# A weight gradient of a strided convolution: fifteen direct tap sums replaced by pairs of taps that share a product

## The chip, the cores and the metric

The program runs on one core of one Trainium2 chip. The metric is the device time of one execution in microseconds (us). Before the change it is 2222.19 us, the median of 4 runs (2219.1 to 2223.2). Lower is better.

The engines have short names here. PE is the matrix engine and PEld its weight loads, DVE the vector engine, ACT the scalar engine, POOL the engine GpSimd, and SP the engine whose queue issues most of the transfers (DMAs).

## The reference, cut to what matters

Two convolutions over time, each with 15 taps, a GELU and a stride of 2, are followed by a small joint network. The kernel computes the output and the gradients of all seven inputs.

```python
def _fwd_reference(x, w1, w2, g, w_f, w_g, w_o):
    B, T, D = x.shape            # 2, 4000, 512
    K = w1.shape[0]              # 15 taps
    pad = K // 2
    ...
    h = _gelu(h)[:, ::2, :]      # first convolution with w1, then every 2nd step
    T1 = h.shape[1]              # 2000
    hp = jnp.pad(h, ((0,0),(pad,pad),(0,0)))
    f = jnp.zeros_like(h)
    for i in range(K):
        f = f + jnp.einsum("btc,cd->btd", hp[:, i:i+T1, :], w2[i])
    f = _gelu(f)[:, ::2, :]      # 1000 steps are kept
    ...
def reference(x, w1, w2, g, w_f, w_g, w_o, grad_out):
    _out, _vjp = jax.vjp(_f, x, w1, w2, g, w_f, w_g, w_o)
    return (_out, *_vjp(grad_out))
```

The change concerns one of these gradients, that of `w2` (output `out_3`, 15 x 512 x 512). With `dy` the gradient before the second GELU (1000 kept steps, 512 channels, 2 batches) it is, for each tap `i`, `gw2[i][c, d] = sum over b, t of hp[b, 2t + i, c] * dy[b, t, d]`: fifteen matrix products that contract over 2 x 1000 time steps.

## The kernel before, in words

The kernel is one long program of five stages: (1) first convolution, (2) second convolution, (3) joint network and its gradients, (4) backward through the second convolution, (5) backward through the first. Stage 4 ends with the gradient of `w2`, and this is the part that changes; it is called the w2 stage here. Stage 5 begins with the gradient of `x` and ends with the gradient of `w1`.

**Order.** The program is written in the order of the stages, but a list scheduler orders the instructions of each engine: it goes through the program with a model of durations, and where the next instruction of an engine isn't ready it puts a later one that is ready before it. On the chip each engine then works its own list in order. Most buffers are blocks of one big SBUF tile (`arena`), given out by a first-fit allocator (`_Arena`, L28); an instruction waits for another where their bytes overlap, so an instruction of a new block waits for the last reader of what lay there before. PSUM has two pools in stage 4, 6 banks for sums (`ps_acc`) and 2 for transposes (`ps_tp`).

**The w2 stage.** The hidden activations `h` lie in DRAM (`HD`), channels on partitions, split by the parity of the time step. `dy` is transposed first: `DFP` (L916 to L928) has 125 groups of 8 consecutive steps, the group on the partition, the step `l` in 0..7 and the 512 channels in the free dimension. Then the stage goes through 8 pieces (L951), 2 parities `par` times 4 blocks of 128 channels `cc`. For each piece:

- `load_htr` (L942) brings 504 KB of `h` into `HTr`, two pieces ahead. The buffers alternate, and the SP queue issues the load.
- `deint` (L167, run by `evac` at L163) rearranges it on ACT to `HTd`, two copies of 128 x 1008.
- 32 transposes on PE (L966) turn it to `HN`, time groups on partitions, 16 positions for each batch; 4 PSUM tiles of 8 transposes are emptied by ACT and DVE in turn (L968).
- For each tap of this parity (8 or 7), 16 matmuls (2 batches x 8 steps, L977) of 125 x 128 by 125 x 512 are summed in one bank. The bank is copied to `st` by ACT or DVE (L981), and `st` is stored to `out_3` by the SP queue (L982).

That is 15 taps x 4 blocks x 16 = 960 matmuls and 8 x 32 = 256 transposes.

**Work of stage 5 that is put in between.** `p5w_setup` (L540) allocates the weight buffers of stage 5 and loads the first quarter of `w1` (1920 KB, L447). POOL then forms 7 sums of taps (L448, L449). `p5w_emit` (L548) transposes a loaded quarter (88 transposes, L460) and loads the next; it is called after pieces 2 and 5. `p5x_load` (L509) loads parts of `x` on POOL's queue for the end of stage 5, as soon as the bytes of its blocks are free.

**The function that the change calls.** Stage 5 computes the gradient of `w1` with `kara_wgrad` (L804). It handles the taps in pairs. For taps `t0` and `t0+2` and for even and odd steps of `dy` it makes three sums instead of four: Q from the unchanged data with `dy` even + odd, P and R from differences of neighbouring data with `dy` even and `dy` odd. Then tap `t0` is P + Q and tap `t0+2` is Q - R. Each sum takes half as many matmuls as a direct tap, since it goes over step pairs. ACT copies Q (L825), DVE adds (L827) and subtracts (L831). Tap 13 is left over and is summed directly from two sums in one bank (L843).

Blocks of the arena at the w2 stage, worked out from the allocator's calls (bytes of a partition): DFP 40192 to 56576, HN 56576 to 72960, HTr 72960 to 81024, st 81024 to 84096, the weights for stage 5 143360 to 210944. The stage before had the G1 tile of batch 1 at 101248 to 117248, read last by L894, and weights at 62720 to 85248, read last by L482. Stage 5 puts the two halves of its `x` data at 68416 to 91968 and 91968 to 115520, and SQ where DFP was.

## Time and profile before

| | us |
|---|---|
| time, median of 4 runs | 2222.19 (2219.1 to 2223.2) |
| the profiled execution, its time | 2217.83 |
| the profiled execution, its span | 2216.1 |
| first and last start of the w2 stage's matmuls (L977) | 1275.2 and 1522.1 |
| first and last start of the matmuls of `kara_wgrad` in stage 5 (L820) | 1891.3 and 2184.7 |
| mean granted PE clock over the span | 0.988 |

The span runs from the first to the last instruction; the time has some 1.7 us more. A group's row names the line, engine and operation, output and input, sizes and count, then busy time, the mean of one in ns and the idle time of the engine before it, with what ended that idle time. A row of the timeline has start, duration, engine, line and tiles, and in brackets the idle time before it. A row of the chain has start, duration and what ran. A row of windows gives, for a stretch, each engine's busy time and count, then the granted clock, the DMA share and GB/s. The line named for a copy or a PSUM emptying is that of the helper (L163 for ACT, L165 for DVE).

### The profile page before, as it was taken

What the parts mean: (1) busy time and instruction counts of PE and PEld (TensorE: products, weight loads), DVE (VectorE), ACT (ScalarE), POOL (GpSimd) and SP (SyncE); (2) the same over time, 40 slices, a digit from 0 to 9 for tenths busy, and PEclk for the clock granted to TensorE, in tenths of its full rate; (3) what the DMA queues carried; (4) which work ended last, traced back from release to release, by engine and by line L of the source; (5) the groups of instructions that cost most, each with busy time, mean ns of one, the idle gap of its engine ahead of it and who ended that gap; (6) DMA issues with size and microseconds to landing.
All of it is one profiled execution on the core that took longest, in us unless ns stands there. A gap on an engine that the chain in (4) does not pass through costs nothing.

```text
span 2216.1 us, 29813 instructions
## 1 busy us (share of the span) xinstructions
PE 2116.0 (95%) x12176; PEld 1077.5 (49%) x12176; DVE 796.1 (36%) x1918; ACT 577.7 (26%) x1141; POOL 478.6 (22%) x416
## 2 busy tenths in 40 slices
PE   5999999999899999999799899999999989999999
PEld 4444444444566656666444444444454444444444
DVE  4333433543455555556354511112222242311310
ACT  2112121121555545552221333221122141000000
POOL 0332232353544444443110011011010000100000
PEclk9999999999999999999899899999999999999999
DMA  7422523743222222224210242113121001600000
GB/s 167 100 62 64 137 55 82 179 97 82 89 75 75 76 77 75 77 72 141 89 36 1 59 120 81 36 65 75 26 56 28 19 19 28 135 24 27 27 24 24
DMA packets 227985, 154.16 MB, mean 70 GB/s; under 512 B 167792, under 2 KB 219412, under 8 KB 223592
## 3 DMA queue, kind: packets, MB, share of 16 engines
q1 hardware_dynamic: 221096, 124.09, 21.6%
q0 software_dynamic: 4288, 11.78, 2.4%
q10 hardware_dynamic: 2464, 16.39, 2.3%
q8 instruction: 95, 1.56, 0.3%
q14 instruction: 42, 0.34, 0.1%
HBM read 100.02 MB, written 52.17 MB: 69 GB/s over the span
## 4 chain that ended last, share of the span: by engine, by line
PE 84%; ACT 7%; DVE 4%; DMA 2%; issue 1%; SPq 1%; POOL 0%; ACTq 0%; DVEq 0%; POOLq 0%
PE acc_l L221 22%; PE acc_gw L977 9%; PE acc_bP L482 7%; PE acc_bQ L482 7%; PE acc_bR L482 6%; PE gwo L695 5%; PE pj L677 5%; PE acc_kP L820 4%; PE acc_kR L820 4%; PE acc_kQ L820 4%; ACT arena L163 4%; ACT arena L628 3%; DVE arena L165 2%; PE tp_wk L460 2%; PE pdfe L688 1%; PE acc_k L843 1%
## 5 line engine op out<-in xcount | busy, mean ns | idle before, releaser
L221 PE MATMUL acc_l<-arena 128*128 128x500 bf16 x2208 | 495.2, 385 | 3.1 <-POOL arena L209 1.6
L221 PEld LDWEIGHTS <-arena 128*128 128x128 bf16 x2208 | 213.2, 97 | 283.8 <-issue 5.2
L482 PEld LDWEIGHTS <-arena 128*128 128x128 bf16 x2208 | 211.7, 97 | 256.1 <-DVE arena L165 1.6
L820 PEld LDWEIGHTS <-arena 125*128 125x128 bf16 x1344 | 131.6, 98 | 163.8 <-issue 5.6
L977 PE MATMUL acc_gw<-arena 125*128 125x512 bf16 x960 | 210.3, 380 | 0.1
L482 PE MATMUL acc_bP<-arena 128*128 128x501 bf16 x768 | 183.9, 385 | 1.1 <-DVE arena L165 1.1
L636 POOL TENSOR_TENSOR arena<-arena 128x500 f32<-128x500 bf16 x128 | 130.7, 1021 | 202.3 <-ACT arena L628 202.2
L482 PE MATMUL acc_bQ<-arena 128*128 128x501 bf16 x768 | 174.1, 375 | 0.0
L628 ACT ACTIVATE arena<-arena 128x125 bf16<-128x125 f32 x512 | 158.8, 400 | 55.1 <-DVE arena L165 55.1
L482 PE MATMUL acc_bR<-arena 128*128 128x501 bf16 x672 | 158.4, 384 | 0.0
L682 DVE SCALAR_TENSOR_TENSOR arena<-arena,pj 128x125 bf16<-128x125 bf16 x512 | 111.7, 282 | 112.7 <-PE pj L677 112.5
L977 PEld LDWEIGHTS <-arena 125*128 125x128 bf16 x960 | 93.5, 98 | 113.4 <-ACT arena L163 2.5
L695 PE MATMUL gwo<-arena 125*128 125x512 bf16 x512 | 141.7, 379 | 0.0
L677 PE MATMUL pj<-arena 128*128 128x500 bf16 x512 | 118.4, 373 | 5.5 <-ACT arena L163 5.4
L448 POOL TENSOR_TENSOR arena<-arena 128x2048 bf16<-128x2048 bf16 x8 | 33.5, 4189 | 386.4 <-DMA arena<-in_w_dram 287.1
L178 POOL TENSOR_TENSOR arena<-arena 128x500 f32<-128x500 f32 x48 | 62.0, 1293 | 252.6 <-ACT arena L175 247.5
L653 PE MATMUL po<-arena 128*125 128x512 bf16 x512 | 113.3, 379 | 0.0
L820 PE MATMUL acc_kQ<-arena 125*128 125x512 bf16 x448 | 103.1, 383 | 2.8 <-DVE arena L1100 2.8
L820 PE MATMUL acc_kP<-arena 125*128 125x512 bf16 x448 | 101.3, 379 | 0.6 <-DVE arena L1127 0.6
L820 PE MATMUL acc_kR<-arena 125*128 125x512 bf16 x448 | 101.3, 379 | 0.0
L1024 DVE TENSOR_TENSOR arena<-arena 128x500 bf16<-128x500 f32 x32 | 22.1, 689 | 214.7 <-ACT arena L1022 214.7
L228 DVE TENSOR_TENSOR arena<-acc_l,arena 128x500 f32<-128x500 f32 x24 | 16.3, 679 | 205.7 <-ACT arena L227 205.7
(137 smaller groups left out, 2223.6 us busy)
## 6 DMA issues: line engine op xcount, KB each, us to landing
arena<-in_w_dram SPq DMA_DIRECT2D x64, 480.0 KB
out_dram<-arena SPq DMA_DIRECT2D x132, 128.0 KB
arena<-in_w_dram SPq DMA_DIRECT2D x8, 1920.0 KB
arena<-in_grad_out_dram SPq DMA_DIRECT2D x16, 896.0 KB
out_dram<-arena ACTq DMA_DIRECT2D x16, 896.0 KB
arena<-in_x_dram POOLq DMA_DIRECT2D x4, 2576.0 KB, 19.5
arena<-in_x_dram SPq DMA_DIRECT2D x8, 896.0 KB
out_dram<-arena SPq DMA_DIRECT2D x64, 112.0 KB
```

The lines of the kernel that those rows point to most:

```text
L163: nc.scalar.copy(out_ap, in_ap)
L178: nc.gpsimd.tensor_tensor(xsq, sm, z, op=ALU.mult)
L221: nc.tensor.matmul(acc[:, :win], WP[:, cc, wi_, :], arr[an][:, cc, par, a0:a0 + 2 * win - 1:2], start=(k == 0), stop=(k == nk - 1))
L482: nc.tensor.matmul(acc[:, :N + 1], WT[:, dc, wi_, :], rhs, start=(k == 0), stop=(k == nk - 1))
L628: nc.scalar.activation(jt[:, ec, u, :], fe[:, ec, :], ACT.Tanh, bias=GE[:, ec, b * U + u:b * U + u + 1])
L636: nc.gpsimd.tensor_tensor(sq, jt[:, :, u, :], jt[:, :, u, :], op=ALU.mult)
L653: nc.tensor.matmul(po[:CH, :D], jt[:, ec, u, :], WO[:, ec, :], start=(ec == 0), stop=(ec == NC - 1))
L677: nc.tensor.matmul(pj[:, :4 * CH], WOT[:, vc, ec * P:(ec + 1) * P], dot[:, vc, 4 * uh:4 * uh + 4, :].rearrange("p u r -> p (u r)"), start= ...
L682: nc.vector.scalar_tensor_tensor(dpre[:, u, :], omj[:, ec, u, :], 1.0, pj[:, ul * CH:(ul + 1) * CH], op0=ALU.mult, op1=ALU.mult, accum_out ...
L695: nc.tensor.matmul(GWO[ec][:, :D], jn[:, u, ec * P:(ec + 1) * P], do[:, u, :], start=(k == 0 and u == 0), stop=(k == nsb_tot - 1 and u == ...
L820: nc.tensor.matmul(acc[:, :D], data(b, comp, kind, l + m, cc), dy(b, dk, l), start=(k == 0), stop=(k == nk - 1))
L977: nc.tensor.matmul(acc[:, :D], HN[:, b, l + off, :], DFP[:, b, l, :], start=(k == 0), stop=(k == nk - 1))
```

## The change

The w2 stage uses `kara_wgrad`, once for each block of 128 channels. What it does:

- The 8 pieces (parity, block) become 4 pieces (block `cc`), each with both parities: one load of 1008 KB for each, two pieces ahead as before.
- DVE, no longer ACT, rearranges (4 copies of 128 x 1008, `UD`), and DVE forms differences of neighbours (`DD`, two subtractions of 128 x 1764 and two of 128 x 250). UD and DD are single buffers.
- 84 transposes for each piece (6 kinds of data x 7 positions x 2 batches, two of the kinds from UD and four from DD) go to `HNK`, in 12 PSUM tiles emptied by ACT and DVE in turn. `HNK` has two buffers.
- `kara_wgrad` gets a list of blocks `ccs`; for one block it makes 7 pairs x 3 sums x 8 matmuls and 16 matmuls for tap 13, so 184, and 736 in all.
- `DYB2`, the sum of even and odd steps of `dy`, is formed at the start by DVE (2 additions of 125 x 2048).
- The first quarter of `w1` is no longer loaded by `p5w_setup`, but in piece 1, behind a small DVE copy of two elements of DD into the weights' buffer, which the load has to wait for. `p5w_emit` is called in pieces 2 and 3, after the piece's transposes and ahead of its matmuls.

Blocks after the change, worked out from the allocator's calls: DD 0 to 8064, DYB2 56576 to 64768, HNK 64768 to 107776, HTr 107776 to 123904, UD 123904 to 131968, seven st and two m2 blocks up to 143232; DFP and the weights for stage 5 stay.

```diff
@@ p5w_setup
-        p5w["WN"] = {0: kbwd_weights_load(w1, 0, nblk)}
+        p5w["WN"] = {}
@@ kara_wgrad
-    def kara_wgrad(ps_pool, data, dy, Lq, out_w, comp_prep, m2_blks, st_blks, scnt0):
+    def kara_wgrad(ps_pool, data, dy, Lq, out_w, comp_prep, m2_blks, st_blks, scnt0, ccs=None):
         scnt = scnt0
-        gcnt = 0
+        gcnt = scnt0
+        ccs = list(range(NC)) if ccs is None else ccs
...
-                for cc in range(NC):
+                for cc in ccs:
...
@@ the w2 stage
-            hn_blks = [AR.alloc(B * LH * P * 2) for _ in range(2)]
-            htd_blks = [AR.alloc(B * L2 * NPH * 2) for _ in range(2)]
-            htr_blks = [AR.alloc(B * TH * 2) for _ in range(2)]
-            st_blks = [AR.alloc(D * 2) for _ in range(3)]
+            Lq2 = L2 // 2
+            NJ2 = Lq2 + 3
+            DYB2_blk, DYB2 = AR.new(BF16, [B, Lq2, D], parts=CH)
+            for b in range(B):
+                v = DFP[:, b].rearrange("p (l par) d -> p l par d", par=2)
+                nc.vector.tensor_tensor(DYB2[:, b], v[:, :, 0, :], v[:, :, 1, :], op=ALU.add)
+            hnk_blks = [AR.alloc(B * 6 * NJ2 * P * 2) for _ in range(2)]
+            dd_blk, DD = AR.new(BF16, [2, B, L2, NPH])
+            htr_blks = [AR.alloc(2 * B * TH * 2) for _ in range(2)]
+            ud_blk, UD = AR.new(BF16, [2, B, L2, NPH])
+            st_blks = [AR.alloc(D * 2) for _ in range(7)]
+            m2_blks = [AR.alloc(D * 4) for _ in range(2)]
...
-                nc.sync.dma_start(v, HD[:, cc, par])
+                nc.sync.dma_start(v, HD[:, cc])
...
-            for gi, (par, cc) in enumerate(gpieces):
...
-                for b in range(B):
-                    deint("act", HTd[:, b], HTr[:, b, :], L2)
...
-                for i in taps:
-                    off = tap_src(i)[1]
-                    acc = ps_acc.tile([P, 512], F32, tag="acc", name="acc_gw2")
...
-                            nc.tensor.matmul(acc[:, :D], HN[:, b, l + off, :], DFP[:, b, l, :],
-                                             start=(k == 0), stop=(k == nk - 1))
...
-                if "p5" in phases and gi in (2, 5):
+            KSRC = [("D", 1, 0), ("U", 1, 1), ("D", 1, 1), ("D", 0, 1), ("U", 0, 2), ("D", 0, 2)]
+            KIDX = {(1, "P"): 0, (1, "Q"): 1, (1, "R"): 2, (0, "P"): 3, (0, "Q"): 4, (0, "R"): 5}
+            for cc in range(NC):
+                HTr = htrs.pop(cc)
+                HNK = AR.view(hnk_blks[cc % 2], BF16, [B, 6, NJ2, P], parts=CH)
+                for par in range(2):
+                    for b in range(B):
+                        deint("dve", UD[:, par, b], HTr[:, par, b, :], L2)
+                if cc + 2 < NC:
+                    htrs[cc + 2] = load_htr(cc + 2)
+                for par in range(2):
+                    nc.vector.tensor_tensor(DD[:, par, :, 0:L2 - 1, :], UD[:, par, :, 0:L2 - 1, :], UD[:, par, :, 1:L2, :],
+                                            op=ALU.subtract)
+                    nc.vector.tensor_tensor(DD[:, par, :, L2 - 1, 0:NPH - 1], UD[:, par, :, L2 - 1, 0:NPH - 1],
+                                            UD[:, par, :, 0, 1:NPH], op=ALU.subtract)
+                if cc == 1 and "p5" in phases:
+                    nc.vector.tensor_copy(AR.view(p5w["wn"][0], BF16, [NW * D])[:, 0:2], DD[:, 1, 1, 0, 0:2])
+                    p5w["WN"][0] = kbwd_weights_load(w1, 0, p5w["wn"][0])
+                ecnt = 0
                 for b in range(B):
...
+                    slots = [(ki, j) for ki in range(6) for j in range(NJ2)]
+                    for s0 in range(0, len(slots), 8):
+                        grp = slots[s0:s0 + 8]
+                        pt = ps_tp.tile([P, 1024], BF16, tag="tp", name="tp_hnk")
+                        for q, (ki, j) in enumerate(grp):
+                            an, par, o = KSRC[ki]
+                            lp = 2 * j + o
+                            src = (UD if an == "U" else DD)[:, par, b, lp % L2, lp // L2:lp // L2 + CH]
+                            nc.tensor.transpose(pt[:CH, q * P:(q + 1) * P], src, ident[:])
+                        evac("act" if ecnt % 2 == 0 else "dve",
+                             HNK[:, b].rearrange("p k j c -> p (k j) c")[:, s0:s0 + len(grp), :],
+                             pt[:CH, :len(grp) * P].rearrange("p (a b) -> p a b", b=P))
+                        ecnt += 1
...
+                if "p5" in phases and cc in (2, 3):
                     p5w_emit(ps_tp)
+                scnt = kara_wgrad(ps_acc, data2, dy2, Lq2, out_3, lambda comp: None, m2_blks, st_blks, scnt, ccs=[cc])
```

Here `data2` gives the transposed kind and position from `HNK`, and `dy2` gives the even steps of `DFP` for A, the odd ones for C and `DYB2` for B.

More of the change, by code (lines that the diff above doesn't have):

```diff
@@ L835, in kara_wgrad @@
             if comp == 0:
-                for cc in range(NC):
+                for cc in ccs:
                     acc = ps_pool.tile([P, 512], F32, tag="acc", name="acc_k13")
@@ L932, in build_kernel @@
                 p5w_setup()
-            LH = L2 + 8
             NPH = TH // L2
-            hn_blks = [AR.alloc(B * LH * P * 2) for _ in range(2)]
-            htd_blks = [AR.alloc(B * L2 * NPH * 2) for _ in range(2)]
-            htr_blks = [AR.alloc(B * TH * 2) for _ in range(2)]
-            st_blks = [AR.alloc(D * 2) for _ in range(3)]
-            scnt = 0
-            gpieces = [(par, cc) for par in range(2) for cc in range(NC)]
-            def load_htr(gi):
-                par, cc = gpieces[gi]
-                v = AR.view(htr_blks[gi % 2], BF16, [B, TH])
-                nc.sync.dma_start(v, HD[:, cc, par])
+            Lq2 = L2 // 2
@@ new lines, in build_kernel, with data2, dy2 @@
+            KSRC = [("D", 1, 0), ("U", 1, 1), ("D", 1, 1), ("D", 0, 1), ("U", 0, 2), ("D", 0, 2)]
[17 more added lines that the diff above has]
+                ecnt = 0
+                for b in range(B):
+                    slots = [(ki, j) for ki in range(6) for j in range(NJ2)]
[11 more added lines that the diff above has]
+                        ecnt += 1
+                def data2(b, comp, kind, j, cc_, HNK=HNK):
+                    return HNK[:, b, KIDX[(comp, kind)], j, :]
+                def dy2(b, kind, l):
+                    if kind == "A":
+                        return DFP[:, b, 2 * l, :]
+                    if kind == "C":
+                        return DFP[:, b, 2 * l + 1, :]
+                    return DYB2[:, b, l, :]
+                if "p5" in phases and cc in (2, 3):
```

30 lines of the change are left out of this document (5 added, 25 removed).

## The prediction

> **What bounds the kernel now.** I read the page's totals first, then its chain of work that ended last.
>
> ```profile
> span 2216.1 us, 29813 instructions
> PE 2116.0 (95%) x12176; PEld 1077.5 (49%) x12176; DVE 796.1 (36%) x1918; ACT 577.7 (26%) x1141; POOL 478.6 (22%) x416
> ...
> PE 84%; ACT 7%; DVE 4%; DMA 2%; issue 1%; SPq 1%; POOL 0%; ACTq 0%; DVEq 0%; POOLq 0%
> ...
> L977 PE MATMUL acc_gw<-arena 125*128 125x512 bf16 x960 | 210.3, 380 | 0.1
> ```
>
> PE holds 84% of the chain, and the matmuls of the w2 stage (L977) wait for 0.1 us in all. The other engines are far from full. So the stage is worth what PE does in it: matmuls, transposes and the gaps between them. The chain around a piece boundary, and the timeline of the same place, show the gaps:
>
> ```profile
> 1327.53 0.48 PE tp_hn L966 x8
> 1328.04 1.02 ACT arena L163
> ...
> 1329.10 1.08 PE tp_hn L966 x16
> 1330.18 1.73 PE acc_gw L977 x8
> ...
> 1464.57 27.63 PE acc_gw L977 x128
> ```
>
> ```profile
> 1329.10 1.08 PE L966 MATMUL tp_hn<-ident,arena 128*125 128x128 bf16 x16 [0.64 <-ACT arena L163]
> ...
> 1331.76 2.00 ACT L163 COPY arena<-arena 128x1008 bf16<-128x1008 bf16 x1
> ```
>
> From the last matmul of a piece (1327.53) to the first of the next (1330.18) 2.65 us pass: 32 transposes, and one wait of 0.64 us until ACT has emptied a transpose tile. The rearranging copy of the piece after (1331.76, on ACT) runs beside the matmuls, long before it is needed: the scheduler pulls such work forward. Idle time of PE in the stage by groups of lines, and the stage's first transposes on PE's timeline:
>
> ```profile
> L966 PE MATMUL tp_hn<-ident,arena 128*125 128x128 bf16 x256 | 19.0, 233 | 8.9 <-ACT arena L163 8.9
> L460 PE MATMUL tp_wk<-ident,arena 128*128 128x128 bf16 x176 | 11.8, 219 | 5.9 <-ACT arena L163 5.9
> ```
>
> ```profile
> 1270.76 1.97 PE L966 MATMUL tp_hn<-ident,arena 128*125 128x128 bf16 x16 [1.78 <-ACT arena L163]
> 1273.55 1.87 PE L966 MATMUL tp_hn<-ident,arena 128*125 128x128 bf16 x16 [0.83 <-ACT arena L163]
> ```
>
> **The change, part by part.** All terms are against this execution.
>
> *Matmuls.* The direct taps run at 27.63 / 128 = 0.216 us from start to start. The chained sums of `kara_wgrad` in stage 5 have the same operands:
>
> ```profile
> 1905.23 3.62 PE L820 MATMUL acc_kQ<-arena 125*128 125x512 bf16 x16
> 1908.69 3.62 PE L820 MATMUL acc_kP<-arena 125*128 125x512 bf16 x16
> ...
> 1925.95 3.62 PE L820 MATMUL acc_kQ<-arena 125*128 125x512 bf16 x16
> ```
>
> Six groups of 16 take 20.72 us, again 0.216 us. 960 matmuls become 736, so **224 x 0.216 = -48.4 us**. This is on the path, since PE has no pause there.
>
> *Transposes.* 256 become 336. By the two rows above one keeps PE busy for 19.0 / 256 = 0.074 us or 11.8 / 176 = 0.067 us; the former includes those at the slow start, so 80 x 0.067 = **+5.4 us**.
>
> *Gaps while transpose tiles are emptied.* Before: 8.9 + 5.9 = 14.8 us, of which 1.78 + 0.83 = 2.6 us fall at the start of the stage, so 12.2. After, each piece has 12 tiles on two banks, so 6 waits of some 0.65 us if nothing fills them: 15.6 us, and with the weights' 5.9 us 21.5. But they can be filled: in the old pieces the first 8 matmuls need the whole first half of HN, while the first new sum (P or Q) needs 4 positions of one kind, there after one or two tiles. Six banks take 24 matmuls of batch 0, 5.2 us, and `p5w_emit` now stands ahead of matmuls that are already fed. That the scheduler weaves transposes into a running sum is seen in stage 5:
>
> ```profile
> 1891.29 4.25 PE L820 MATMUL acc_kQ<-arena 125*128 125x512 bf16 x11 [2.80 <-DVE arena L1100]
> ...
> 1895.38 1.09 PE L1076 MATMUL tp_dx<-ident,arena 128*125 128x128 bf16 x16
> ...
> 1896.30 1.24 PE L820 MATMUL acc_kQ<-arena 125*128 125x512 bf16 x5
> ```
>
> I take two unfilled waits for each piece, 4 x 1.3 = 5.2 us: **-7.0 us**. The bounds are 0 and 21.5 us unfilled, so -12.2 to +9.3.
>
> *Start of the stage.* The front of the first piece can't be hidden. The timeline of DVE there, and DVE's groups for its price:
>
> ```profile
> 1261.57 1.27 DVE L894 TENSOR_TENSOR arena<-arena 128x500 bf16<-128x500 f32 x1
> ...
> 1269.01 0.69 DVE L165 COPY arena<-tp_dfp 125x1024 bf16<-125x1024 bf16 x1 [0.16 <-PE tp_dfp L926]
> ```
>
> ```profile
> L165 DVE COPY arena<-tp_dfp 125x1024 bf16<-125x1024 bf16 x8 | 5.5, 696 | 4.0 <-issue 2.2 <-PE tp_dfp L926 1.8
> L165 DVE COPY arena<-arena 128x1000 bf16<-128x1000 bf16 x4 | 4.0, 1044 | 1.4 <-PE acc_bQ L482 1.4
> ...
> L1127 DVE TENSOR_TENSOR arena<-arena 125x5632 bf16<-125x5632 bf16 x2 | 6.2, 3086 | 4.2 <-PE acc_bQ L482 4.2
> ```
>
> Before, the first transposes of the stage start at 1270.76, right after the ACT copy. Now they need four copies and four subtractions on DVE, which is busy with the emptying of `tp_dfp` until 1269.70. A copy is 1.044 us, so 4.2 us. A subtraction goes at 3086 / 5632 = 0.55 ns an element: 2 x 1764 and 2 x 250 elements, the small ones unaligned and taken at twice that rate, 2.5 us. One DYB2 addition (2048 elements) adds 1.1 us. DVE is through at 1269.7 + 7.8 = 1277.5, so the front comes **+7 us** later. The load isn't earlier than this by much: its block now lies where G1 was, which L894 reads until 1262.84. Windows show what the first two loads of 504 KB took before, when nothing else was on the way:
>
> ```profile
> 1256.00:1259.00 3.00, 1.64 (x22) 1.48 (x23) 2.09 (x4) 0.68 (x2) 0.00 (x0) 1.00 0.79 255
> 1259.00:1262.00 3.00, 1.01 (x8) 0.82 (x7) 3.00 (x5) 0.69 (x1) 0.00 (x0) 0.67 0.25 97
> ```
>
> 255 and 97 GB/s over 3 us each are the 1.03 MB, so about 5 us, and the first 1008 KB are there by 1268, hidden behind DVE. The bounds: DVE has 4.0 us of gaps between the emptyings, which copies may use (+3), and half of the kinds need only one parity's subtraction (+1); and a load as late as the worst one seen, by the list of waits,
>
> ```profile
> ACT arena L163 <- DMA arena<-HD: 11.9, 1, 11.9
> ```
>
> puts it at +7 + 6 = +13, if half of that wait is covered by DVE's other work. The loads of `w1` and of half of `x` that made it late are now behind this place.
>
> *The clock* is halved while PE is thinly used, before as after:
>
> ```profile
> 1274.00:1277.00 3.00, 3.00 (x19) 1.90 (x18) 0.69 (x1) 3.00 (x3) 0.00 (x0) 0.50 1.05 285
> 1277.00:1280.00 3.00, 3.00 (x15) 1.34 (x14) 0.00 (x0) 1.19 (x1) 0.00 (x0) 0.98 1.04 255
> ```
>
> It came back some 6.3 us after the first transposes (1270.76 to 1277), which costs half of that, 3.2 us. I take it as the same now: nothing in the sum. The Trainium skill, "TensorE: Matmul & The Clock Gate", Part 1, says that the matrix engine falls to half its rate after an idle window of about 3.4 us and regains it after a busy one. The rows agree, with a longer return than that; by the page the sum would be the same too.
>
> *The end of the stage.*
>
> ```profile
> 1521.86 1.11 DVE arena L1007
> 1522.98 0.61 DVE arena L165
> 1523.59 0.05 issue
> ```
>
> PE waits 1.8 us here, since the last sum is emptied by DVE (0.61) behind an addition of stage 5 (1.11). After the change ACT empties the last one (tap 13), with nothing ahead of it, in about the same 0.6 us: **-1.0 us** (0 to -1.5).
>
> *What is hidden.* DVE's front of pieces 1 to 3 (4.2 + 2.5 us) lies beside some 40 us of matmuls: UD and DD are free once the piece's transposes are through, and HNK has a second buffer. For a pair of taps PE takes 24 x 0.216 = 5.2 us, and behind it DVE runs two operations and ACT one, for which stage 5 has rows:
>
> ```profile
> L827 DVE TENSOR_TENSOR arena<-acc_kP,arena 128x512 bf16<-128x512 f32 x28 | 19.3, 691 | 150.8 <-PE acc_kP L820 150.8
> ```
>
> So 1.4 us of DVE in 5.2, with six banks; a copy of 1 us put between delays no sum. If that cover fails, it costs 6.7 us a boundary. The load of `w1` waits behind DD of piece 1; SP's later stores and loads stand behind it only in its queue. What it takes is shown by the second such load, on SP's and POOL's timeline:
>
> ```profile
> 1362.92 0.39 SPq L447 DMA_DIRECT2D arena<-in_w_dram  x1
> ...
> 1371.01 4.06 POOL L448 TENSOR_TENSOR arena<-arena 128x2048 bf16<-128x2048 bf16 x1 [74.16 <-DMA arena<-in_w_dram]
> ...
> 1375.02 3.10 POOL L449 TENSOR_TENSOR arena<-arena 128x1536 bf16<-128x1536 bf16 x1
> ```
>
> From issue to the last sum 15.2 us. DD of piece 1 is due about 10 us after the first piece's transposes, and piece 2 begins some 80 us after them; the second quarter has the 40 us of piece 2's matmuls. Both are covered. The half of `x` that was loaded at the start of the stage now waits for its end, as its block holds HNK and HTr; its first reader comes some 360 us later, ahead of the first L820 at 1891, and this costs nothing.
>
> POOL's sums are also the one place for a rule that speaks against the change. The Trainium skill, "SBUF — State Buffer", section "Who interferes with whom", says that a DVE instruction with two SBUF inputs and a GpSimd instruction that reads SBUF block each other. The row of L744, where one operation is shared out to both engines, agrees:
>
> ```profile
> L744 DVE TENSOR_TENSOR arena<-arena x4: 677/896/2784, 962.2 to 1028.9; 128x504 bf16<-128x504 bf16 x4
> ```
>
> The same 504 elements took DVE 0.68 to 2.78 us. By the page the subtractions of a piece could be held up for POOL's 7.2 us; that falls in the 40 us of cover, and the sum stays.
>
> **Sum.** -48.4 + 5.4 - 7.0 + 7 - 1.0 = **-44 us**, so 2173.8 us against this execution's 2217.83. Its span is 2216.1, and 1.7 us lie around it as before. The median of the runs shown, 2222.19, is 4.4 us above it; against the median I predict **2178 us**. With the gap term at -10 to -3 and the start at +3 to +13 the forecast's own range is 2171 to 2188.
>
> **The rivals.**
>
> *The gaps are not filled.* The weaving in stage 5 speaks against it, the bare gaps of the weights' transposes before (5.9 us) for it. Then the gap term is +9.3 in place of -7.0: -27.7 us, 2194.5.
>
> *DVE's front lies open at the boundaries*, because the scheduler puts it behind the last sums of the piece. It would cost 3 x 6.7 = 20 us: 2198 with filled gaps, and with unfilled ones too 2214.5. The early ACT copy at 1331.76 speaks against it; for it only that UD and DD are single.
>
> *Slower than before.* One mechanism, at the three inner boundaries: the front lies open, so the gaps are bare (+16.3) and DVE's 6.7 us count (+20), PE idles so long that the clock halves each time (3 x 3.2), and POOL's 7.2 us of sums of the weights, issued just then, hold up the subtractions (3 x 7.2 = 21.6). -44 + 67.5 = +23.5, so 2246. It is slower once each boundary loses some 16 us more than forecast. Against it: POOL has only two or three such sums in the stage, and at the old boundary with 120 transposes and bare gaps the clock stayed up:
>
> ```profile
> 1354.00:1366.00 12.00, 7.55 (x111) 6.54 (x110) 4.58 (x7) 7.40 (x9) 0.00 (x0) 1.00 0.20 61
> ```
>
> *It doesn't do what it says:* the matmuls fall, but stage 5 waits instead, for `x` data that come later, and nothing is left. The data have those 360 us; hardly possible.
>
> **How the numbers follow.** Forecast 57%, gaps bare 19%, front open 10%, both 7%, slower 5%, nothing left 2%. The first three hold 86%. The range takes the forecast's lowest bounds together (-48.4 + 5.4 - 12.2 + 1 - 1.5 = -55.7) and reaches up to the open front with the 2 us by which the runs differ from their median: 2166 to 2200. A difference under 0.2% (4.4 us) can hardly be told from none here. Faster by more than that: 57 + 19 + 10 + 7 = 93%; within 2%; slower 5%.
>
> **What the next profile would show.** Some 168 matmuls a piece at L820 and 16 at L843, 736 in the stage, 0.216 us apart; the stage's first transposes near 1277; copies of 128 x 1008 on DVE in mid-piece; at the boundaries transposes in eights with sums between them, and idle time before them near 5 us in all; the first matmul of stage 5 near 1479. Wrong it would be if DVE copies stood at the boundaries, if PE waited for DMA or POOL ahead of L460, or if the 44 us came back as idle time later.

## The result, and the profile after

| | before | after |
|---|---|---|
| time, median | 2219.26 us (12 runs, 2215.77 to 2223.81) | 2173.96 us (8 runs, 2167.31 to 2174.93) |
| ratio, with its 95% interval | | 0.9788 (0.9777 to 0.9798) |
| the profiled execution, its time | 2217.83 us | 2173.22 us |
| the profiled execution, its span | 2216.1 us | 2171.4 us |

The change makes the kernel 45.3 us faster by the medians and 44.7 us by the spans; 2178 (2166 to 2200) was forecast. The page's totals and its chain's shares, after:

```profile
span 2171.4 us, 29575 instructions
...
PE 2076.3 (96%) x12032; PEld 1062.9 (49%) x12032; DVE 844.5 (39%) x1987; ACT 556.5 (26%) x1135; POOL 476.8 (22%) x416
...
PE 85%; ACT 5%; DVE 5%; DMA 2%; issue 1%; SPq 1%; POOL 0%; ACTq 0%; DVEq 0%; POOLq 0%
```

PE is busy for 39.7 us less, DVE for 48 us more, and DVE's share of the chain rises by one point only. The work that DVE took over is nearly all hidden. Where the time went is read from two stretches: from the first transposes of the w2 stage to the first sum of stage 5 (L482), and from there to the first matmul of the gradient of `w1`. The view of windows gives for each the length, then each engine's busy time; before (first transposes at 1270.76):

```profile
1270.76:1523.64 252.88, 238.63 (x1393) 121.36 (x1393) 43.00 (x62) 72.51 (x73) 29.12 (x22) 0.99 0.25 73
1523.64:1891.29 367.65, 358.75 (x2016) 173.03 (x2017) 106.08 (x141) 85.93 (x103) 18.76 (x20) 1.00 0.17 36
```

and after (first transposes at 1276.78):

```profile
1276.78:1477.10 200.32, 195.53 (x1249) 104.80 (x1250) 81.08 (x123) 53.44 (x68) 30.10 (x22) 0.99 0.28 89
1477.10:1846.45 369.35, 361.59 (x2017) 175.28 (x2016) 106.24 (x141) 85.97 (x103) 20.62 (x24) 0.99 0.18 38
```

The first stretch is 52.6 us shorter: 43.1 us of PE's busy time and 9.5 us of its idle time (252.88 - 238.63 = 14.25 before, 200.32 - 195.53 = 4.79 after). The first transposes come later: 20.92 us behind the first `tp_dfp` in place of 15.30 (1255.86 and 1255.46), so 5.6 us of the 52.6 are given back. That leaves 46.9 us. The second stretch, where nothing was changed, is 1.7 us longer in this execution; the last section takes that up.

The groups of PE's instructions in the stage, after, show what is left of the idle time (the last number, with what ended it):

```profile
L821 PE MATMUL acc_kQ<-arena 125*128 125x512 bf16 x224 | 57.5, 383 | 0.0
...
L987 PE MATMUL tp_hnk<-ident,arena 128*125 128x128 bf16 x336 | 26.9, 232 | 11.2 <-DVE arena L970 7.5 <-ACT arena L163 2.2 <-DVE arena L165 1.1
L844 PE MATMUL acc_k<-arena 125*128 125x512 bf16 x64 | 14.5, 379 | 0.0
L460 PE MATMUL tp_wk<-ident,arena 128*128 128x128 bf16 x176 | 11.8, 218 | 0.4 <-DVE arena L165 0.3
```

The sums wait for nothing. The weights' transposes (L460), which waited 5.9 us before, wait 0.4. The new transposes wait 11.2 us, 7.5 of them once, at the start, for DVE's subtraction (L970). At a boundary between pieces, PE's and ACT's timeline after:

```profile
1325.18 1.09 PE L987 MATMUL tp_hnk<-ident,arena 128*125 128x128 bf16 x16
1325.38 0.58 ACT L163 CAST arena<-acc_k 128x512 bf16<-128x512 f32 x1 [6.28 <-PE acc_k L844]
1325.86 1.02 ACT L163 COPY arena<-tp_hnk 125x1024 bf16<-125x1024 bf16 x1
...
1326.93 0.62 PE L987 MATMUL tp_hnk<-ident,arena 128*125 128x128 bf16 x8 [0.66 <-ACT arena L163]
...
1327.39 0.38 PE L821 MATMUL acc_kQ<-arena 125*128 125x512 bf16 x1
...
1327.90 0.62 PE L987 MATMUL tp_hnk<-ident,arena 128*125 128x128 bf16 x8
```

One wait of 0.66 us is bare. From the third transpose tile on, single matmuls of a sum (1327.39) stand between the transposes, so the emptying of a tile is nearly covered: two waits follow at this boundary, of 0.27 and 0.17 us.

### The profile page after: what moved, and what is told of

It is laid out like the page before. It is cut to its first block, busy times and chain, and to the rows that moved or that the text cites. A ratio compares the mean times of both kernels' runs of the same rounds, so it can differ in the third digit from the quotient of the medians.

```text
span 2171.4 us, 29575 instructions
## 1 busy us (share of the span) xinstructions
PE 2076.3 (96%) x12032; PEld 1062.9 (49%) x12032; DVE 844.5 (39%) x1987; ACT 556.5 (26%) x1135; POOL 476.8 (22%) x416
## 4 chain that ended last, share of the span: by engine, by line
PE 85%; ACT 5%; DVE 5%; DMA 2%; issue 1%; SPq 1%; POOL 0%; ACTq 0%; DVEq 0%; POOLq 0%
PE acc_l L221 22%; PE acc_bP L482 7%; PE acc_bQ L482 7%; PE acc_kR L821 7%; PE acc_bR L482 7%; PE acc_kP L821 6%; PE acc_kQ L821 6%; PE gwo L695 5%; PE pj L677 5%; DVE arena L165 3%; ACT arena L628 3%; ACT arena L163 2%; PE acc_k L844 2%; PE tp_wk L460 2%; PE pdfe L688 1%; PE po L653 1%
## 5 line engine op out<-in xcount | busy, mean ns | idle before, releaser
L482 PEld LDWEIGHTS <-arena 128*128 128x128 bf16 x2208 | 212.1, 97 | 255.8 <-issue 1.6
L821 PEld LDWEIGHTS <-arena 125*128 125x128 bf16 x2016 | 196.1, 98 | 234.7 <-issue 5.5
L482 PE MATMUL acc_bP<-arena 128*128 128x501 bf16 x768 | 183.9, 385 | 0.7 <-ACT arena L163 0.7
L482 PE MATMUL acc_bQ<-arena 128*128 128x501 bf16 x768 | 174.8, 376 | 0.0
L821 PE MATMUL acc_kQ<-arena 125*128 125x512 bf16 x672 | 160.4, 383 | 2.8 <-DVE arena L1120 2.8
L482 PE MATMUL acc_bR<-arena 128*128 128x501 bf16 x672 | 158.8, 384 | 0.0
L821 PE MATMUL acc_kP<-arena 125*128 125x512 bf16 x672 | 155.8, 379 | 0.8 <-DVE arena L1147 0.8
L821 PE MATMUL acc_kR<-arena 125*128 125x512 bf16 x672 | 155.5, 379 | 0.0
L826 ACT COPY arena<-acc_kQ 128x512 f32<-128x512 f32 x56 | 32.8, 586 | 363.7 <-PE acc_kQ L821 353.2
L828 DVE TENSOR_TENSOR arena<-acc_kP,arena 128x512 bf16<-128x512 f32 x56 | 38.7, 691 | 215.8 <-PE acc_kP L821 213.3
```

Source lines behind the costliest of these rows:

```text
L482: nc.tensor.matmul(acc[:, :N + 1], WT[:, dc, wi_, :], rhs, start=(k == 0), stop=(k == nk - 1))
L821: nc.tensor.matmul(acc[:, :D], data(b, comp, kind, l + m, cc), dy(b, dk, l), start=(k == 0), stop=(k == nk - 1))
```

## The experiments

Each ratio, with its 95% interval, is to the kernel before in the same group of runs, whose median was 2218.99 to 2220.31 us. A difference from the changed kernel is one of medians of different groups. A profile's "stage" is from the first `tp_dfp` to the first L482 of stage 5 (268.18 us before, 221.24 after). It is finer than the time here, since runs of one kernel differ by 2 to 11 us.

| kernel | time, us | ratio to before | first transposes, behind first `tp_dfp` | stage, us |
|---|---|---|---|---|
| after | 2173.96 | 0.9788 (0.9777 to 0.9798) | 20.92 | 221.24 |
| after, run again | 2173.05 | 0.9785 (0.9772 to 0.9799) | 20.99 | 220.57 |
| direct taps on the new front | 2210.0 | 0.9954 (0.9939 to 0.9969) | 18.06 | 259.32 |
| front held open | 2194.8 | 0.9886 (0.9866 to 0.9906) | 21.00 | 244.55 |
| weights' transposes behind the sums | 2182.57 | 0.9833 (0.9818 to 0.9849) | 20.90 | 233.23 |
| `w1` loaded early | 2176.95 | 0.9809 (0.9787 to 0.983) | 21.00 | 224.66 |
| front reordered | 2166.92 | 0.9765 (0.975 to 0.978) | 15.96 | 214.86 |
| one HNK buffer | 2168.95 | 0.9772 (0.9757 to 0.9787) | 17.40 | 217.44 |
| two HNK, one placed last | 2170.65 | 0.9773 (0.976 to 0.9787) | 17.39 | 217.57 |
| other blocks for UD, DD, HTr | 2163.86 | 0.9746 (0.9732 to 0.9759) | 13.40 | 212.07 |
| three transpose banks | 2169.61 | 0.9774 (0.9759 to 0.979) | 20.31 | 217.69 |
| reordered + three banks | 2164.7 | 0.9752 (0.9735 to 0.9768) | 16.31 | 213.11 |
| other blocks + subtractions ahead + three banks | 2159.04 | 0.9722 (0.9708 to 0.9735) | 12.38 | 207.96 |

### Do the matmuls carry the gain? Direct taps on the new front

The front (load, copies, differences) stays; the sums are the old ones, 960 matmuls, fed by 256 transposes of UD. DD is formed and not read.

```diff
-                    slots = [(ki, j) for ki in range(6) for j in range(NJ2)]
+                    slots = [(par, lp) for par in (1, 0) for lp in range(L2 + 8)]
...
-                scnt = kara_wgrad(ps_acc, data2, dy2, Lq2, out_3, lambda comp: None, m2_blks, st_blks, scnt, ccs=[cc])
+                for i in [t for t in range(KT) if t % 2 == 0] + [t for t in range(KT) if t % 2 == 1]:
+                    par, off = tap_src(i)
...
+                    for b in range(B):
+                        for l in range(L2):
+                            nc.tensor.matmul(acc[:, :D], HN[:, b, 1 - par, l + off, :], DFP[:, b, l, :],
```

> Keeps the new pieces (both parities at once, four of them, copies on DVE, weights transposed ahead of the piece's matmuls) but sums the fifteen taps directly: 960 matmuls and 256 transposes in place of 736 and 336. My theory (PE-bound, the matmuls carry the gain): against the changed kernel +224 x 0.216 = +48.4 for the matmuls, -80 x 0.067 = -5.4 for the transposes, -2.5 for the subtractions that the first piece doesn't wait for: +40 us, so 2214 us, still about 5 us under the kernel before, since gaps are filled. Rival (the gain comes from the new order of the pieces and the filled gaps, the matmuls were hidden or limited elsewhere): within 15 us of the changed kernel, under 2190.

Measured: 36 us slower than the changed kernel, the stage 38.1 us longer. So the fewer matmuls carry most of the gain; that the order and the buffers carry it has fallen. Yet the stage is still 8.9 us shorter than before, with as many matmuls and transposes. PE's groups of this kernel show from where:

```profile
L985 PE MATMUL tp_hnk<-ident,arena 128*125 128x128 bf16 x256 | 19.0, 230 | 7.1 <-DVE arena L165 4.5 <-ACT arena L163 2.3
L460 PE MATMUL tp_wk<-ident,arena 128*128 128x128 bf16 x176 | 12.2, 218 | 0.2
```

The weights' transposes no longer wait, 0.2 us in place of 5.9: they now stand ahead of matmuls that are already fed. The transposes inside the pieces wait 2.6 us (7.1 less the 4.5 at the start) in place of 6.3 (8.9 less 2.6). That part of the change has nothing to do with the shared products.

### Is DVE's front hidden? The front held open

Four copies of two elements tie UD to the stored tile of tap 13, the last of a piece, so that the next piece's copies can't start before the piece ends. The values are overwritten by the copies that follow.

```diff
+                if cc > 0:
+                    last = AR.view(st_blks[(scnt - 1) % len(st_blks)], BF16, [D])
+                    for par in range(2):
+                        for b in range(B):
+                            nc.vector.tensor_copy(UD[:, par, b, 0, 0:2], last[:, 0:2])
```

> In pieces 1 to 3, four small DVE copies that read the stored tile of tap 13 of the piece before are put ahead of DVE's copies to UD, so that DVE's front can only start when the sums before it are through. My theory (the front is hidden in the changed kernel and costs its length where it isn't): for each boundary 4 copies of 1.06, subtractions 2.7, small copies 0.6 and the emptying 0.6, 8.2 us, so +25 us, 2199. Rival with the clock (PE idles about 8 us each time and comes back at half rate for some 6 us): +25 + 3 x 3.2 = +35, 2209, with a granted clock of 0.5 behind each boundary. Rival (not hidden in the changed kernel either): 0.

Measured: 20.8 us slower than the changed kernel, the stage 23.3 us longer. PE's timeline of this kernel at the first boundary, and the windows there (the number behind POOL's is the granted clock):

```profile
1331.12 1.97 PE L992 MATMUL tp_hnk<-ident,arena 128*125 128x128 bf16 x16 [6.88 <-DVE arena L975]
```

```profile
1324.00:1334.00 10.00, 2.88 (x25) 2.56 (x24) 7.34 (x14) 1.60 (x2) 0.00 (x0) 0.75 0.42 135
1334.00:1337.00 3.00, 3.00 (x27) 2.24 (x26) 0.81 (x2) 1.25 (x2) 0.00 (x0) 0.68 1.09 371
1337.00:1340.00 3.00, 3.00 (x39) 2.37 (x37) 0.86 (x2) 2.07 (x3) 0.17 (x1) 1.00 0.71 223
```

PE is idle for 6.88 us at the first boundary (6.88 and 6.87 at the two others), where the prediction had 6.7 for an open front. The clock dips behind it, until 1337, and PE is busy for 5.4 us more in all (200.94 us from the first transposes to L482, 195.53 in the changed kernel). Against that the transposes wait 2.7 us less for the emptying of their tiles. Together that is the 23.3. In the changed kernel nothing of this is to be seen, so there the front is hidden.

### What fills the weights' gaps? Their transposes behind the sums

```diff
-                if "p5" in phases and cc in (2, 3):
-                    p5w_emit(ps_tp)
                 scnt = kara_wgrad(ps_acc, data2, dy2, Lq2, out_3, lambda comp: None, m2_blks, st_blks, scnt, ccs=[cc])
+                if "p5" in phases and cc in (1, 2):
+                    p5w_emit(ps_tp)
```

> The two calls that transpose weights of stage 5 go from between a piece's transposes and its matmuls to the end of the piece before, as in the old kernel; they fall at the same two boundaries. My theory (the old bare gaps were 5.9 us, now 0.4, because fed matmuls fill them): +5.5 us, 2179.5, with 5 to 6 us of idle time of PE before L460. Rival (the place of the call makes no difference, the scheduler finds other work): 0 us.

Measured: 8.6 us slower, the stage 12.0 us longer. The expected part is there, in PE's groups of this kernel:

```profile
L987 PE MATMUL tp_hnk<-ident,arena 128*125 128x128 bf16 x336 | 26.5, 229 | 15.9 <-DVE arena L970 7.5 <-DVE arena L165 4.6 <-ACT arena L163 3.7
...
L460 PE MATMUL tp_wk<-ident,arena 128*128 128x128 bf16 x176 | 11.8, 219 | 6.0 <-ACT arena L163 6.0
```

L460 waits 6.0 us in place of 0.4. The part that was missed is the 4.7 us more at L987. Some 1.5 us of it (3.7 against 2.2, behind ACT) also come from the place of the call: the first transposes of a piece now stand bare behind those of the weights. The other part is a single place. The timeline at the second boundary shows it, POOL, DVE and PE together:

```profile
1387.81 4.24 POOL L448 TENSOR_TENSOR arena<-arena 128x2048 bf16<-128x2048 bf16 x1 [79.09 <-DMA arena<-in_w_dram]
...
1388.64 4.35 DVE L970 TENSOR_TENSOR arena<-arena 128x1764 bf16<-128x1764 bf16 x1
...
1392.02 3.92 POOL L449 TENSOR_TENSOR arena<-arena 128x1536 bf16<-128x1536 bf16 x1
...
1393.52 3.35 DVE L165 COPY arena<-arena 128x1008 bf16<-128x1008 bf16 x1
1393.65 0.27 PE L987 MATMUL tp_hnk<-ident,arena 128*125 128x128 bf16 x2 [3.13 <-DVE arena L165]
```

The earlier call frees the weights' buffer earlier, so the next load of `w1` lands earlier, and POOL's sums now meet DVE's work for the next piece. A subtraction that takes 1.07 us elsewhere takes 4.35, a copy of 1.06 takes 3.35. Both end 0.9 us behind POOL's instruction that they met (1392.99 and 1392.05, 1396.87 and 1395.94): they look as if they stood until POOL was through. DVE also empties transpose tiles, and PE waits 3.13 us for one. So the place of the call was worth some 7 us (5.6 and 1.5) by itself, and a collision of some 3 us came on top. The rest of the 12.0 is busy time of PE, 197.18 us in place of 195.53.

### Does it matter that `w1` is loaded late?

```diff
-        p5w["WN"] = {}
+        p5w["WN"] = {0: kbwd_weights_load(w1, 0, nblk)}
...
-                if cc == 1 and "p5" in phases:
-                    nc.vector.tensor_copy(AR.view(p5w["wn"][0], BF16, [NW * D])[:, 0:2], DD[:, 1, 1, 0, 0:2])
-                    p5w["WN"][0] = kbwd_weights_load(w1, 0, p5w["wn"][0])
```

> The load of the first quarter of w1 (1920 KB) goes back to the start of the stage, without the small copy that held it. My theory: the first load of h is issued ahead of it and lands in time for DVE's first copy, so 0 to +2 us, 2174 to 2176. Rival (the loads share the DMA engines, and the first piece is late): +4 to +8 us, with DVE waiting for HD before its first copy.

Measured: the time is 3 us above the changed kernel's, the intervals overlap; the stage is 3.4 us longer. Neither theory gave the cause. DVE didn't wait for the load of `h`, and the first transposes come no later (21.00 us). The timeline of this kernel right behind them:

```profile
1271.71 7.13 POOL L448 TENSOR_TENSOR arena<-arena 128x2048 bf16<-128x2048 bf16 x1 [123.92 <-DMA arena<-in_w_dram]
...
1277.19 2.58 DVE L165 COPY arena<-arena 128x1008 bf16<-128x1008 bf16 x1
...
1278.80 3.93 POOL L449 TENSOR_TENSOR arena<-arena 128x1536 bf16<-128x1536 bf16 x1
...
1280.29 3.36 DVE L165 COPY arena<-arena 128x1008 bf16<-128x1008 bf16 x1
...
1283.89 1.09 PE L984 MATMUL tp_hnk<-ident,arena 128*125 128x128 bf16 x16 [2.54 <-DVE arena L165]
```

The same collision: POOL's first sum comes 30 us earlier than in the changed kernel, meets DVE's subtractions and takes 7.13 us in place of 4.06. The subtractions keep their pace here (2.08 us for two); DVE's copies of piece 1 behind them take 2.58 and 3.36 and end 0.9 us behind POOL's sums. PE waits 2.54 us for DVE. So the load behind piece 1 is worth some 3 us, through POOL and not through the DMA queue.

### What holds up the start? Order of the front

Parity 1 first, each parity's subtractions right behind its copies, the additions of DYB2 behind them, and ACT takes half of the first piece's copies.

```diff
-                for par in range(2):
+                for par in (1, 0):
                     for b in range(B):
-                        deint("dve", UD[:, par, b], HTr[:, par, b, :], L2)
-                if cc + 2 < NC:
-                    htrs[cc + 2] = load_htr(cc + 2)
-                for par in range(2):
+                        deint("act" if cc == 0 and b == 1 else "dve", UD[:, par, b], HTr[:, par, b, :], L2)
                     nc.vector.tensor_tensor(DD[:, par, :, 0:L2 - 1, :], UD[:, par, :, 0:L2 - 1, :], UD[:, par, :, 1:L2, :],
...
+                if cc == 0:
+                    emit_dyb2()
```

> The order of the front: the odd parity's copies and subtractions first (the sums of the first half need only these), the even parity's behind them, the additions of dy last; in piece 0 ACT makes the copies of batch 1. My theory (the start of the stage is DVE's chain, 7.5 us of idle PE): the first transposes start 4 to 5 us earlier, 2169.5. Rival (the start is set by the load of h or the transposes of dy): 0 us.

Measured: 7 us faster than the changed kernel, the stage 6.4 us shorter; the first transposes come 5.0 us earlier. The start was limited by DVE's own work and its order, as the prediction had it; what each of the three changes is worth was not told apart. Once they are made, ACT waits 2.9 us for the load of `h`, which lands some 5 us after its issue (1266.24 to 1271.19), as the prediction had estimated.

### What holds up the load? The blocks

The first try was meant for something else: whether the second buffer of HNK hides anything.

```diff
-            hnk_blks = [AR.alloc(B * 6 * NJ2 * P * 2) for _ in range(2)]
+            hnk_blks = [AR.alloc(B * 6 * NJ2 * P * 2)]
...
-                HNK = AR.view(hnk_blks[cc % 2], BF16, [B, 6, NJ2, P], parts=CH)
+                HNK = AR.view(hnk_blks[0], BF16, [B, 6, NJ2, P], parts=CH)
```

> One buffer for the transposed data HNK instead of two. My theory (the transposes of a piece stand behind the sums of the piece before anyway, so that the second buffer hides little): 0 to +2 us, 2174 to 2176. Rival (the second buffer is what hides the boundary, as the prediction put it): +3 us or more at three boundaries, 9 us in all.

Measured: 4 to 5 us faster, the stage 3.8 us shorter; neither theory had a gain. From the first transposes to the end of the stage it is the same to 0.3 us (217.44 - 17.40 = 200.04, and 200.32), so the second buffer hides nothing. The gain lies ahead of them, on DVE's timeline:

```profile
1204.16 2.98 DVE L165 COPY arena<-arena 128x1008 bf16<-128x1008 bf16 x3 [4.80 <-DMA arena<-HD]
...
1219.53 1.07 DVE L165 COPY arena<-arena 128x1008 bf16<-128x1008 bf16 x1
```

Three of the rearranging copies run 50 us before the stage, the fourth 35 us before it. In the changed kernel the first of them starts at 1269.11. What it waits for in the changed kernel is seen on DVE's and SP's timeline there:

```profile
1261.96 1.27 DVE L895 TENSOR_TENSOR arena<-arena 128x500 bf16<-128x500 f32 x1
...
1263.26 11.84 SPq L953 DMA_DIRECT2D arena<-HD  x3
```

L895 (L894 before the change), the last reader of G1, ends at 1263.23, and the load is issued at 1263.26. With 21504 bytes fewer ahead of them, HTr moves from byte 107776 to 86272 and UD to 102400, away from what L895 reads last (the last quarter of G1, 113248 to 117248). To tell the address from the number of buffers, the next kernel has two buffers again, the second allocated last:

```diff
-            hnk_blks = [AR.alloc(B * 6 * NJ2 * P * 2) for _ in range(2)]
+            hnk_blks = [AR.alloc(B * 6 * NJ2 * P * 2)]
...
+            hnk_blks.append(AR.alloc(B * 6 * NJ2 * P * 2))
```

> Two buffers of HNK as in the changed kernel, but the second one is allocated last, so that HTr, UD and DD lie where they lay with one buffer. My theory (with one buffer the kernel was faster only because HTr and UD moved to bytes that are free earlier, so that DVE's copies ran before the stage): as with one buffer, 2169 to 2170, first transposes about 17.4 us behind the first transposes of dy in place of 20.9. Rival (a second buffer costs something of itself): 2174.

Measured: first transposes 17.39 us behind `tp_dfp`, stage 217.57 us, the same as with one buffer (17.40 and 217.44). It is the address and not the number of buffers. The time, 2170.65, is some 2 us above that kernel's; its second stretch was one of the long ones (369.31 us).

With one buffer and DD moved too, copies and subtractions of the first piece can run ahead of the stage. A block of UD's size first fills the hole at byte 0 and is given back afterwards, so UD, DD and HTr follow HNK directly:

```diff
+            gap_blk = AR.alloc(2 * B * L2 * NPH * 2)
+            ud_blk, UD = AR.new(BF16, [2, B, L2, NPH])
             dd_blk, DD = AR.new(BF16, [2, B, L2, NPH])
             htr_blks = [AR.alloc(2 * B * TH * 2) for _ in range(2)]
-            ud_blk, UD = AR.new(BF16, [2, B, L2, NPH])
+            AR.release(gap_blk)
```

> One buffer of HNK, and UD, DD and the first HTr put on bytes whose last readers (the G1 tile of batch 0 and three quarters of that of batch 1) are through long before the stage. My theory: copies and subtractions of piece 0 run before the stage, the first transposes follow those of dy or fill their gaps, 12 us earlier than in the changed kernel against the transposes of dy, and the half-clock stretch shrinks with the idle time: -8 to -12 us, 2162 to 2166. Rival (the start is then set by the transposes and copies of dy, which gain nothing): like one buffer, 2169.

Measured: 2163.86, some 9 to 10 us below the changed kernel, the stage 9.2 us shorter. DVE's timeline of this kernel:

```profile
1226.08 3.94 DVE L165 COPY arena<-arena 128x1008 bf16<-128x1008 bf16 x4 [4.82 <-DMA arena<-HD]
...
1241.38 2.07 DVE L972 TENSOR_TENSOR arena<-arena 128x1764 bf16<-128x1764 bf16 x2
```

The whole front of the first piece is done 12 us before `tp_dfp`. The transposes come 7.5 us earlier and not 12, since `tp_dfp` itself is next on PE: they start right behind it.

### The rest of the gaps: a third transpose bank, and all together

```diff
-            ps_acc = es.enter_context(tc.tile_pool(name="ps4_acc", bufs=6, space=PSUM))
-            ps_tp = es.enter_context(tc.tile_pool(name="ps4_tp", bufs=2, space=PSUM))
+            ps_acc = es.enter_context(tc.tile_pool(name="ps4_acc", bufs=5, space=PSUM))
+            ps_tp = es.enter_context(tc.tile_pool(name="ps4_tp", bufs=3, space=PSUM))
```

> Three PSUM banks for transposes and five for sums in stage 4, in place of two and six. My theory: the 3.7 us of waits of the transposes inside the pieces shrink to about 1, -2.5 us, 2171.5. Rival (five banks hold up the sums of the gradient of h earlier in the stage, which need three at a time): slower by some us, with waits at L482 before 1255.

Measured: 4.3 us faster, the stage 3.6 us shorter. Five banks for the sums do: the sums still wait for nothing. With the reordered front:

> Both together, the order of the front and three banks for transposes. My theory: the two gains add up, since one lies at the start of the stage and the other at its boundaries: -7 us, 2167. Rival: one of them is nothing, -2.5 or -4.5.

Measured: 2164.7, the stage 8.1 us shorter, where the two alone had 6.4 and 3.6, so the gains add up to four fifths. Last, the other blocks with three banks, and each parity's subtractions behind its copies, parity 1 first:

> The layout of the kernel beside it, the odd parity's front first, and three PSUM banks for transposes. My theory: another 3.5 us from the waits of the transposes, 2159 to 2162, the fastest of all. Rival (with the transposes of dy and of the first piece interleaved, five banks for sums become the bound): no better than the layout alone.

Measured: **2159.04 us, ratio 0.9722 (0.9708 to 0.9735)**, the fastest of all, some 61 us below before and 14 to 15 below the change. PE's groups of this kernel:

```profile
L988 PE MATMUL tp_hnk<-ident,arena 128*125 128x128 bf16 x336 | 23.1, 222 | 2.3 <-DVE arena L165 1.0 <-ACT arena L163 0.8
...
L460 PE MATMUL tp_wk<-ident,arena 128*128 128x128 bf16 x176 | 11.6, 219 | 0.5 <-DVE arena L165 0.3
```

Of the 11.2 us of waiting ahead of the transposes 2.3 are left. One more run repeated the changed kernel:

> The changed kernel once more, unchanged, beside the three others of this group, as their yardstick: 2174 us, 0.979 of the kernel before. From the first transposes of its w2 stage to the first sum of stage 5 its profile should again show 200 us.

Measured: 2173.05, the stage 220.57 us.

## Why the prediction was right, step by step

**Matmuls and transposes.** -48.4 and +5.4, together -43.0; PE's busy time in the stretch fell by 43.1; only the sum of the two is measured. The chain of the changed kernel has the sums at the expected pace, eight in 1.73 us, 0.216 us each:

```profile
1290.81 1.73 PE acc_kQ L821 x8
1292.53 1.73 PE acc_kP L821 x8
...
1321.89 3.45 PE acc_k L844 x16
```

The group of the transposes alone would say +7.9 (26.9 against 19.0). But now many of them stand between matmuls and overlap them, and such time counts twice in the groups; the busy time in windows counts it once.

**Gaps and end.** Forecast -7.0 and -1.0. Idle time went from 14.25 to 4.79, so -9.5. The end term was misread. The 1.8 us were two instructions of DVE, but PE still worked beside the first of them; PE's own rows there, before and after, have a wait of 1.11 and one of 0.67 us, so -0.4:

```profile
1523.64 3.72 PE L482 MATMUL acc_bP<-arena 128*128 128x501 bf16 x16 [1.11 <-DVE arena L165]
```

```profile
1477.10 3.71 PE L482 MATMUL acc_bP<-arena 128*128 128x501 bf16 x16 [0.67 <-ACT arena L163]
```

The gap term was mis-sized: two unfilled waits a piece, 5.2 us, were taken. PE waits 3.7 us in all ahead of L987 once the start is left out, and 0.4 ahead of L460, so about one and a half a piece, and the term is 4.1 - 12.2 = -8.1. The remaining -0.8 is the wait of 0.83 us at the old start (1273.55), which was in no term. The filling of the weights' gaps, argued from stage 5, was shown by the kernel that took it away (6.0 us).

**Start.** +7 forecast, +5.6 measured; the first transposes were expected at 1277.5 and stand at 1276.78, the first matmul of stage 5 at 1479 and stands at 1477.10. They follow the first large subtraction of each parity and don't wait for the small ones. DVE's timeline, after:

```profile
1269.11 1.03 DVE L165 COPY arena<-arena 128x1008 bf16<-128x1008 bf16 x1
...
1271.62 1.22 DVE L941 TENSOR_TENSOR arena<-arena 125x2048 bf16<-125x2048 bf16 x1
1272.75 2.00 DVE L165 COPY arena<-arena 128x1008 bf16<-128x1008 bf16 x2
1274.67 2.06 DVE L970 TENSOR_TENSOR arena<-arena 128x1764 bf16<-128x1764 bf16 x2
```

The single durations held: 1.03, 1.22 and 1.03 us, where 1.04, 1.1 and 0.97 (1764 x 0.55 ns) were taken. That the load of the first piece is hidden was right for this order only. What the prediction treated as given, the block that G1's last reader holds, was what forced all of this into the open: at another address the copies and subtractions of the first piece cost nothing: the first transposes then come 13.40 us behind `tp_dfp`, before the change 15.30.

**Hidden work.** The front of pieces 1 to 3 is hidden, and an open one costs what was worked out. But one named cover was wrong: the second buffer of HNK hides nothing.

**POOL against DVE.** The prediction weighed the rule of the Trainium skill ("SBUF — State Buffer", "Who interferes with whom") for subtractions only, and left the sum as it was, since the delay would fall in the 40 us of cover. The sum held, but for a reason that was not given: the late load puts POOL's sums into the middle of a piece, where the timeline of the changed kernel has the first one undisturbed:

```profile
1302.05 4.06 POOL L448 TENSOR_TENSOR arena<-arena 128x2048 bf16<-128x2048 bf16 x1 [151.98 <-DMA out_dram<-arena]
```

Two experiments moved them away from there, and where they met DVE's work PE waited some 3 us more each time. So the cover of 40 us doesn't hold by itself: DVE also empties the transpose tiles, and PE waits for these. The same section of the Trainium skill also names copies of one operand, in DVE's fast modes, as work that blocks or is blocked for whole instructions. The copy that grew from 1.06 to 3.36 us was held up like that; whether it ran in such a mode no run here shows.

**The rivals.** Bare gaps fell by the 4.8 us of idle time that are left; the open front by the timeline at the boundary, and by the kernel that has it; the slower case with both. "It doesn't do what it says" fell by the second stretch, which is within 1.7 us of the old one.

**The level.** 2217.83 - 44 = 2173.8 was the sum against the profiled execution, which took 2173.22 after. 2178 came from the first four runs' median, 2222.19; with 12 runs it is 2219.26. That the sum is met to within 1 us is partly luck: the stage itself gained 46.9 us, 3 more than forecast (the gaps, the start and 0.8 that no term had gave more, the end gave less), and 1.7 us were lost behind it in this execution.

## What to carry to other kernels

When an engine's sums wait for nothing, cut its instructions, and then look at the start and the boundaries, where the new helper work may stand bare. In a kernel whose buffers are reused bytes of one block, ask of each first load whose last reader it waits for: three blocks at other addresses (and one buffer less) gave 9 us here. And before a load is moved, look at what it triggers: a transfer that lands earlier may start sums on POOL beside DVE's copies, and DVE's instructions took up to four times as long here.

## What the runs showed of the hardware that was not expected

- DVE and POOL held each other up even where DVE only copied one operand: a copy of 128 x 1008 took 2.58 to 3.36 us beside POOL's sums in place of 1.06, a subtraction of 128 x 1764 took 4.35 in place of 1.07, and POOL's sum of 128 x 2048 took 7.13 in place of 4.06. The four DVE instructions that were held up ended 0.9 us behind the POOL instruction that they met, which is nearly their own undisturbed length: they look held for the whole of it, not slowed.
- The unchanged stretch of stage 5 comes in two lengths, 367.2 to 368.1 us in most profiles and 368.9 to 369.4 in a few, the changed kernel's among them. The windows show a lower granted clock there, in the changed kernel and then in its repetition:

```profile
1755.00:1760.00 5.00, 4.23 (x30) 2.73 (x29) 2.67 (x2) 5.00 (x3) 0.00 (x0) 0.78 0.00 0
...
1765.00:1770.00 5.00, 3.95 (x34) 3.06 (x35) 1.51 (x3) 3.48 (x4) 0.00 (x0) 0.75 0.00 0
```

```profile
1755.00:1760.00 5.00, 3.44 (x33) 2.04 (x30) 2.97 (x3) 4.54 (x2) 0.00 (x0) 1.00 0.04 9
...
1765.00:1770.00 5.00, 3.38 (x38) 2.58 (x39) 2.20 (x4) 4.06 (x5) 0.00 (x0) 1.00 0.00 0
```

  The same program has 0.78 and 0.75 in one execution and 1.00 in the other, and the stretch is 369.35 and 367.59 us long. The three other long ones have such a dip too (0.91 over 20 us). So these 1.7 us are no cost of the change. The Trainium skill, "TensorE: Matmul & The Clock Gate", Part 1, says that the window of activity isn't aligned with the program's start; that would fit, but no run here shows the window itself.
- After 6.9 us without work between dense sums the clock was back some 6 us after the first transposes (0.68 until 1337, 1.00 behind it). It cost less than the 3.2 us a boundary that the prediction's slower case had for it: PE was busy for 5.4 us more in all, 1.8 a boundary, and since waits of the transposes fell away at the same time, 2.7 us are left of it in the stage (23.3 - 3 x 6.88).
